# A planned attention stage: ten softmax norms on GpSimd, no mask products on TensorE, and a planner that ranks steps anew

## The chip, the core and the metric

One core of a Trainium2 chip runs the kernel. The metric is device microseconds (us) from the start to the end of one execution. Three runs of the kernel before took 621.08, 620.10 and 620.14 us, a median of 620.14.

## The reference

Three blocks follow one another, all in float32, for a batch of 4 and 576 positions:

```python
scores = scale * q @ k^T                       # 8 heads of 64
mask = (rel >= 0) & (rel < 64)                 # each position sees itself and 63 before it
attn = softmax(where(mask, scores, -1e9));  x = attn @ v            # x: 4 x 576 x 512

h = relu(x @ w_in);  u, vv = halves of h       # 512 -> 1024
vn = (vv - mean) / sqrt(var + 1e-6)            # over the 512 channels
x = (u * (w_spatial @ vn + b_spatial)) @ w_out

u = x + (relu(x^T @ w_tok1) @ w_tok2)^T
out = u + relu(u @ w_ch1) @ w_ch2              # 512 -> 1536 -> 512
```

The weights arrive as 8-byte floats and are turned into float32 on the chip, from their two 4-byte words.

## The kernel before

Matrix products of float32 quality are made of three products of halves: each operand is split into a rounded high part, made by ScalarE (a CAST), and a remainder, made by VectorE (a subtraction). So each tile that TensorE makes costs a ScalarE and a VectorE step before TensorE can use it again.

Attention runs in 18 turns (`its`), nine for each pair of batches; a turn holds 128 query rows of all 8 heads, and its softmax comes in two halves `g` of four heads. The steps of a turn, with the letters that the planner has for them: S, the scores on TensorE (`scores`, line 264); M, the row maxima on VectorE (`smax`, line 290); X, the exponentials with row sums on ScalarE (`sexp`, line 303); N, the reciprocal of the sums and the multiplication by it on VectorE (`snorm`, line 309); T, four transposes on TensorE (line 488); C, the copy of the transposed half out of the matmul bank on ScalarE (line 489); V, the product with the values (line 324); xh and xl, its split (lines 538 and 543).

For turns 0 to 5 (`MASK_PE = 6`) the mask is added by TensorE: a bf16 product of the identity with the mask (line 278) opens each of the two score banks, M is a reduction (line 294) and a scaling (line 301), and X reads the bank. For the others a fused VectorE instruction (line 297) adds the mask, writes the masked scores to SBUF and takes the minimum of the negated row; X then reads SBUF.

Behind the attention stand the first block's products: v and u (`uv_v_mm`, `uv_u_mm`) from the split x, with a ReLU (R, E), for v the normalisation (bn, rs on GpSimd, ts) and a split (hi, lo), then s, the spatial product, and G, its product with u (line 406). The weights `w_in` come in eight parts of 512 KB (four v, four u); each is loaded (wL), scaled by ScalarE (wd, line 136), joined by VectorE (wo, lines 439 and 440), and split (wh, line 443, and wl, line 445), all in a matmul bank that is held from wd to wl. Spatial, output and channel weights have like steps (`ws_load`, `wo_work`, `c2_work`); the last stores its halves to DRAM.

All of these are steps of a planner (`plan`, class `Steps`). Each step names its engine, a rank, a time in us, a hold (how long the engine is taken), the steps that it comes after, and what it takes and gives of rooms: `sp` (4 score banks), `xo`, `mm` (3 banks), `pb` (3 tiles of probabilities), `PT`, `v`, `qk`, `XT` and others. Steps with a `line` keep their order in that line. The planner simulates: it finds the engine and the earliest time at which some step can start, takes the step with the lowest rank among those of that engine that can start by then, and emits its instructions. So it fixes the order of instructions on each engine; the engines then run in that order and wait for one another with semaphores. Some 217 us of the run are planned in this way.

What follows is written out by hand: the other spatial products, the output product `W`, the token block (`T`, `A`, `tok2`), and the channel block in the form of seven products in place of eight (`ch1_seven`, `product`), with the preparation of weights in time slots beside it (`Line`, `bg`).

Of the kernel before, what the change touches and what calls it, by code (L numbers as in the profile page):

```python
# [25 lines left out]
MASK_PE = 6  # L26
# [3 lines left out]
PAIRS = 4  # L30
DOWN = 2.0 ** -112
# [7 lines left out]
class Steps:  # L39
# [5 lines left out]
    def __init__(self, **room):  # L45
        self.room = {k: [0.0] * n for k, n in room.items()}
        self.clock, self.done, self.open, self.lines = {}, {}, [], {}
        self.pad, self.queue, self.lands = 0, 0.0, [0.0] * 8
# [5 lines left out]
    def start(self, step):  # L54
        name, eng, rank, us, fn, after, take, give, hold, kb = step
        at = self.clock.get(eng, 0.0)
        for a in after:
            if a not in self.done:
                return None
            at = max(at, self.done[a] + self.LAG)  # L60
        for r in set(take):
            free, n = sorted(self.room[r]), take.count(r)
            if len(free) < n:
                return None
            at = max(at, free[n - 1] + self.LAG)
        return max(at, self.lands[-8 + (kb > 520)]) if kb else at

    def run(self):
        while True:
# [10 lines left out]
            gap = at - self.clock.get(eng, 0.0)  # L80
            self.pad = int((gap - 0.5) / 0.3) if PAD and eng == "PE" and gap > 0.8 and at < PAD else 0
# [16 lines left out]
def tile_kernel(ctx, tc, qT, kT, kE, v, w_in, wsT, b_sp, w_out, w_t1, w_t2, w_c1, w_c2, outT):  # L98
# [347 lines left out]

    def wu_part(ft):
        fs = slice(128 * ft, 128 * ft + 128)
        return w_part(U[:, ft, :1024], w_in[:, fs].rearrange("(k p) c -> p k c", p=P), wi_h[:, :, fs], wi_l[:, :, fs], 128)
# [10 lines left out]
    def plan():  # L460
# [11 lines left out]
        def attend(n):  # L472
# [8 lines left out]
            def turned(g):  # L481
# [7 lines left out]
                copies[n, g] = lambda: nc.scalar.copy(out=PT[0][:, 4 * g:4 * g + 4, :], in_=pt)  # L489

            for g in range(2):
                S.add(("M", n, g), "DVE", 1 + n / 100, 0.95, lambda g=g: smax(n, g), after=[("S", n)], give=free * (n >= MASK_PE))
                S.add(("X", n, g), "ACT", 2 + n / 100, 1.65, lambda g=g: sexp(n, g), after=[("M", n, g)], give=free * (n < MASK_PE), hold=1.54)
                S.add(("N", n, g), "DVE", 1 + n / 100, 1.15, lambda g=g: snorm(n, g), after=[("X", n, g)], hold=1.05)
                S.add(("T", n, g), "PE", 1 + n / 100, 0.65, lambda g=g: turned(g), after=[("N", n, g)], take=free + ["PT"] * (g == 0), give=["pb"] * g, line=("T", n), hold=0.45)
                S.add(("C", n, g), "ACT", 1, 0.6, lambda g=g: copies.pop((n, g))(), after=[("T", n, g)], give=free, hold=0.49)
# [7 lines left out]
        def score(n, after, line):  # L504
            S.add(("S", n), "PE", 0, 1.2 + 0.6 * (n < MASK_PE), lambda: scores(n), after=after + [("Lq", n), "ident"],
                  take=[] if after else ["sp", "sp", "pb"], give=["qk"], hold=1.0 + 0.6 * (n < MASK_PE), line=line)

        def block(ns):
# [16 lines left out]
            for m in ns:  # L525
                S.add(("V", m), "PE", 0, 1.25, lambda m=m: product(m), after=[("V", n)] if m > n else need,
                      take=take if m == n else [], give=["v", "PT"], hold=1.05, line=("B", n))
            for m in ahead:
                score(m, [("V", n)], ("B", n))
            for m in ns:  # L530
                S.add(("xh", m), "ACT", 0, 0.6, lambda m=m: xhigh(m), after=[("V", m)], hold=0.49)
                S.add(("xl", m), "DVE", 0, 0.7, lambda m=m: xlow(m), after=[("xh", m)], give=["mm" if m > n else "xo"], hold=0.6)
# [12 lines left out]
        def v_work(p, i):  # L545
# [15 lines left out]
            S.add(("v", n), "PE", 10, 2.9, product, after=[("xl", n)] + [("wl", "v", k) for k in range(4)], take=["mm"], hold=2.75, line="work")  # L561
            S.add(("R", n), "ACT", 1.5, 0.6, relu, after=[("v", n)], take=["vf"], give=["mm"], hold=0.49)
            S.add(("bn", n), "DVE", 2, 0.9, part, after=[("R", n)])
            S.add(("rs", n), "POOL", 0, 1.0, part, after=[("bn", n)])
            S.add(("ts", n), "DVE", 2, 0.56, part, after=[("rs", n)])
            S.add(("hi", n), "ACT", 4, 0.6 if i else 2.2, part, after=[("ts", n)])
            S.add(("lo", n), "DVE", 3, 0.7 if i else 1.3, part, after=[("hi", n)], give=["vf"])

        def u_work(p, c, ft):
            g = {}  # L570

            def product():
# [3 lines left out]
            S.add(("u", p, c, ft), "PE", 10, 2.25, product, after=[("xl", 9 * p + 3 * c + k) for k in range(3)] + [("wl", "u", ft)],  # L576
                  take=["mm"], give=["XT"] * (ft == 3), hold=2.09, line="work")
            S.add(("E", p, c, ft), "ACT", 1.5, 0.5 if c == 2 else 0.72, lambda: uv_u_out(p, c, ft, g["ps"]), after=[("u", p, c, ft)], give=["mm"])

        def s_work(b, d, c0):  # L580
# [8 lines left out]
            S.add(("s", b, d, c0), "PE", 10, 2.0, product, after=tiles + [("ws", k, c0) for k in range(6)], take=["mm"], hold=1.86, line="work")  # L589
            S.add(("G", b, d, c0), "DVE", 0.5, 0.47, lambda: spatial_out(b, d, c0, g["ps"]),  # L590
                  after=[("s", b, d, c0)] + [("E", p, c, d) for c in range(2 + b % 2)], give=["mm"], hold=0.4)

        def w_load(kind, k):
            it = (wv_part if kind == "v" else wu_part)(k)

            def part():
                next(it, 0)

            S.add(("wL", kind, k), "SP", 0, 0, part, hold=0.47, kb=512, line="SP")
            S.add(("wd", kind, k), "ACT", 1.8 if kind == "v" else 2.5, 0.7, part, after=[("wL", kind, k)], take=["mm"], hold=0.6)  # L600
            S.add(("wo", kind, k), "DVE", 0.8 if kind == "v" else 2.5, 1.25, part, after=[("wd", kind, k)])
            S.add(("wh", kind, k), "ACT", 1.8 if kind == "v" else 2.5, 0.6, part, after=[("wo", kind, k)], hold=0.49)
            S.add(("wl", kind, k), "DVE", 0.8 if kind == "v" else 2.5, 0.7, part, after=[("wh", kind, k)], give=["mm"], hold=0.6)

        def ws_load(k, c):
# [8 lines left out]
            S.add(("wh", k, c), "ACT", 3, 0.45, part, after=[("Lw", k, c)], hold=0.35)  # L614
            S.add(("ws", k, c), "DVE", 2.5, 0.45, part, after=[("wh", k, c)], give=["raw"], hold=0.38)
# [41 lines left out]
        def c2_work(j):  # L657

            rank = 6 + j
# [650 lines left out]
```

## Time and profile before

| what | value |
|---|---|
| median of three runs | 620.14 us |
| profiled execution | 621.39 us, of which the span is 619.5 us |
| busy: TensorE, VectorE, ScalarE, GpSimd | 97%, 76%, 57%, 19% of the span |
| mean granted clock of TensorE | 0.991 |
| instructions | 12149 |

The span is the time from the first to the last instruction that the profiler recorded. An engine is busy while it executes; waiting for a semaphore is idle time. TensorE's matmuls overlap one another, so its busy share can hide slow stretches; the number of matmuls in a stretch tells more. PE is TensorE, DVE VectorE, ACT ScalarE, POOL GpSimd, SP the engine that issues the DMAs.

### The profile page before, as it was taken

What the parts mean: (1) busy time and instruction counts of PE and PEld (TensorE: products, weight loads), DVE (VectorE), ACT (ScalarE), POOL (GpSimd) and SP (SyncE); (2) the same over time, 40 slices, a digit from 0 to 9 for tenths busy, and PEclk for the clock granted to TensorE, in tenths of its full rate; (3) what the DMA queues carried; (4) which work ended last, traced back from release to release, by engine and by line L of the source; (5) the groups of instructions that cost most, each with busy time, mean ns of one, the idle gap of its engine ahead of it and who ended that gap; (6) DMA issues with size and microseconds to landing.
All of it is one profiled execution on the core that took longest, in us unless ns stands there. A gap on an engine that the chain in (4) does not pass through costs nothing.

```text
span 619.5 us, 12149 instructions
## 1 busy us (share of the span) xinstructions
PE 600.2 (97%) x4396; PEld 560.6 (90%) x4396; DVE 472.6 (76%) x1066; ACT 352.7 (57%) x889; POOL 114.7 (19%) x145
## 2 busy tenths in 40 slices
PE   4999999999999989999999999999999999999997
PEld 2678899889988989788988999999999999999997
DVE  5998878968888836586278778888875989866982
ACT  5996786766777532674344454546443557544540
POOL 3000202302422200041025212140011140011320
PEclk8899999999999999999999999999999999999999
DMA  8956356866565652415200524665534674444752
GB/s 325 342 187 188 124 198 228 262 225 223 203 203 180 229 179 69 137 57 167 84 34 35 170 69 169 221 224 168 184 126 173 230 234 159 153 137 170 237 197 77
DMA packets 49812, 108.05 MB, mean 174 GB/s; under 512 B 4948, under 2 KB 17496, under 8 KB 49752
## 3 DMA queue, kind: packets, MB, share of 16 engines
q1 hardware_dynamic: 49752, 107.27, 51.2%
q8 instruction: 35, 0.57, 0.4%
q14 instruction: 25, 0.20, 0.1%
HBM read 86.81 MB, written 20.45 MB: 173 GB/s over the span
## 4 chain that ended last, share of the span: by engine, by line
PE 62%; DVE 4%; DMA 4%; ACT 2%; issue 1%; POOL 0%; ACTq 0%
PE A L1167 19%; PE mm L183 13%; PE mm L955 12%; PE A L955 9%; PE A L183 6%; DMA scr<-raw 3%; PE A L873 1%; DMA craw<-in_w_out 1%; PE A L1251 1%; DVE pb L297 1%; DVE raw L689 0%; ACT raw L686 0%; DVE pb L316 0%; DVE st L372 0%; DVE hid L949 0%
## 5 line engine op out<-in xcount | busy, mean ns | idle before, releaser
L1167 PE MATMUL A<-room,w 128*128 128x384 f32 x720 | 131.1, 335 | 0.7 <-DVE U L1203 0.7
L1167 PEld LDWEIGHTS A<-room,w 128*128 128x128 f32 x720 | 125.1, 188 | 2.1 <-DVE U L1203 1.0
L1161 ACT CAST room<-hid 128x384 fp32r<-128x384 f32 x120 | 61.3, 513 | 48.9 <-PE A L1167 37.5
L1162 DVE TENSOR_TENSOR room<-hid,room 128x384 fp32r<-128x384 f32 x120 | 71.9, 625 | 13.9 <-ACT room L1161 12.2
L949 POOL TENSOR_TENSOR hid<-hid 128x384 f32<-128x384 f32 x36 | 44.2, 1239 | 202.8 <-DVE hid L949 160.0
L183 PE MATMUL mm<-ws,room 128*128 128x288 f32 x416 | 61.0, 297 | 1.6 <-DVE U L406 1.5
L183 PEld LDWEIGHTS mm<-ws,room 128*128 128x128 f32 x416 | 56.7, 188 | 2.6 <-DVE U L406 2.1
L980 ACT ACTIVATE hid<-hid 128x384 f32<-128x384 f32 x54 | 28.1, 525 | 42.4 <-DVE hid L983 42.4
L983 DVE TENSOR_TENSOR hid<-A,hid 128x384 f32<-128x384 f32 x54 | 29.5, 554 | 24.7 <-PE A L955 18.4
L306 ACT ACTIVATE pb<-pb,nm 128x128 f32<-128x128 f32 x96 | 37.2, 392 | 2.8 <-DVE nm L297 2.8
L955 PE MATMUL mm<-room,sh 128*128 128x384 f32 x144 | 37.2, 334 | 0.0
L183 PE MATMUL mm<-xh,wi_h 128*128 128x384 f32 x96 | 33.2, 346 | 0.0
L183 PE MATMUL mm<-xh,wi_l 128*128 128x384 f32 x96 | 32.2, 336 | 0.0
L183 PE MATMUL mm<-xl,wi_h 128*128 128x384 f32 x96 | 32.2, 335 | 0.0
L1192 DVE TENSOR_TENSOR U<-A,U 128x384 f32<-128x384 f32 x42 | 21.9, 551 | 11.1 <-PE A L1167 6.5
L183 PE MATMUL mm<-gh,wo_h 128*128 128x512 f32 (+1 forms) x80 | 30.2, 378 | 0.0
L183 PE MATMUL mm<-gl,wo_h 128*128 128x512 f32 (+1 forms) x80 | 29.6, 370 | 0.2 <-DVE gl L855 0.2
L813 POOL TENSOR_TENSOR k<-k 128x256 f32<-128x256 f32 x12 | 9.7, 832 | 107.1 <-ACT gh L854 59.4
L183 PE MATMUL mm<-gh,wo_l 128*128 128x512 f32 (+1 forms) x80 | 29.5, 369 | 0.0
L855 DVE TENSOR_TENSOR gl<-U,gh 128x512 fp32r<-128x512 f32 (+1 forms) x20 | 13.3, 667 | 21.1 <-ACT gh L854 21.0
L488 PE MATMUL sp<-ident,pb 128*128 128x128 f32 x144 | 21.7, 284 | 7.0 <-DVE pb L316 3.0
L170 ACT CAST sh<-k 128x1024 fp32r<-128x1024 f32 x18 | 18.9, 1050 | 15.7 <-PE mm L955 5.9
(181 smaller groups left out, 1546.0 us busy)
## 6 DMA issues: line engine op xcount, KB each, us to landing
w<-scr SPq DMA_DIRECT2D x63, 512.0 KB, 4.1
scr<-raw SPq DMA_DIRECT2D x48, 256.0 KB, 3.5
k<-sums SPq DMA_DIRECT2D x18, 512.0 KB, 3.8
kk<-in_kT SPq DMA_DIRECT2D x16, 384.0 KB, 5.5
craw<-in_w_c SPq DMA_DIRECT2D x24, 256.0 KB, 3.7
qq<-in_qT SPq DMA_DIRECT2D x18, 256.0 KB, 5.5
va<-in_v SPq DMA_DIRECT2D x18, 256.0 KB, 4.4
vb<-in_v SPq DMA_DIRECT2D x18, 256.0 KB, 4.6
```

The lines of the kernel that those rows point to most:

```text
L170: nc.scalar.copy(out=hi, in_=x)
L183: nc.tensor.matmul(o, a, c, start=(i == 0), stop=(i == n - 1))
L306: nc.scalar.activation(out=pb[:, h, :], in_=scs[g][:, h - 4 * g, :] if mk is None else pb[:, h, :], func=AF.Exp, scale=SCALE if mk is None ...
L488: nc.tensor.transpose(pt[:, h, :], pb[:, 4 * g + h, :], ident)
L949: eng.tensor_tensor(out=out, in0=a, in1=b, op=ALU.subtract)
L955: nc.tensor.matmul(o, a, m, start=first and i == 0, stop=i == len(todo) - 1, skip_group_check=True)
L980: nc.scalar.activation(out=o, in_=src, func=AF.Relu)
L983: nc.vector.tensor_tensor(out=o, in0=a, in1=b, op=ALU.add)
L1161: nc.scalar.copy(out=oh, in_=blk[j])
L1162: nc.vector.tensor_tensor(out=ol, in0=blk[j], in1=f(oh), op=ALU.subtract)
L1167: nc.tensor.matmul(acc[d], a, m, start=(first and j == 0 and i == 0), stop=(last and j == NJ - 1 and i == 2), skip_group_check=True)
L1192: nc.vector.tensor_tensor(out=at, in0=src, in1=at, op=ALU.add)
```

## The change

The mask product goes from TensorE for all turns (`MASK_PE = 0`), so turns 0 to 5 have the fused VectorE instruction too. For turns 0 to 9 (`EARLY`) the multiplication by the reciprocal sum is done by GpSimd; the reciprocal stays on VectorE and becomes a step I of its own. For half 0 of turn 0 and half 1 of turns 3 to 7 (`CD0`, `CD1`) VectorE makes the copy C in place of ScalarE. One part of the u weights (`PU`) is prepared in place in SBUF, without a matmul bank, and its remainder is made by GpSimd. The order of the first fourteen loads changes (`ORDER`). In the planner all ranks are replaced by a table, several times and holds are changed, a step comes `SLACK` later behind the steps that it waits for (not behind rooms), and TensorE's clock in the simulation is charged `SWITCH` when it goes from one shape of matmuls to another. The hand-written part isn't changed.

```diff
-MASK_PE = 6
+MASK_PE = 0
+EARLY = range(0, 10)
+CD0 = range(0, 1)
+CD1 = range(3, 8)
+PU = (1,)
+ORDER = (0, 2, 5, 4, 3, 1, 7, 6, 10, 9, 8, 12, 13, 11)
+RANK = dict(M=0.96, X=5.22, I=-0.72, N=6.15, T=0.48, C=1.04, xh=3.48, xl=-0.6, R=0.29, bn=3.08, ts=0.44, hi=4.2, lo=5.8, E=1.49, G=-4.23, av=3.48, dv=1.82, au=4.89, du=3.49, aw=2.75, dw=1.67, c2=4.58)
+SLACK = dict(cd=0.38, cs=0.3, ch=2.95, cl=0.35, oh=0.73, ol=0.69, aw=2.46, ws=2.23, sums=0.17, wd=0, X=0, N=0.3, T=0.32, C=0.14, xh=0.03, xl=0.01, R=0.6, bn=1.03, ts=0.21, hi=0.54, lo=1.64, E=0.9, G=0.2)
+SHAPE = dict(S="score", V="pv")
+SWITCH = {(None, "pv"): 0.14, ("pv", "score"): 0.17, ("score", None): 0.28, ("pv", None): 0.16, (None, "score"): 0.2, ("score", "pv"): 0.14}
...
+        lag = self.LAG + SLACK.get(name[0], 0.0)
...
-            at = max(at, self.done[a] + self.LAG)
+            at = max(at, self.done[a] + lag)
...
+            if eng == "PE":
+                shape = SHAPE.get(name[0])
+                at += SWITCH.get((self.shape, shape), 0.0)
+                self.shape = shape
...
-        nc.vector.tensor_tensor(out=pb[:, hs, :], in0=pb[:, hs, :], in1=rs.unsqueeze(2).to_broadcast([P, w, 128]), op=ALU.mult)
+        yield
+        eng = nc.gpsimd if n in EARLY else nc.vector
+        eng.tensor_tensor(out=pb[:, hs, :], in0=pb[:, hs, :], in1=rs.unsqueeze(2).to_broadcast([P, w, 128]), op=ALU.mult)
...
+    def wu_pool(ft):
+        fs = slice(128 * ft, 128 * ft + 128)
+        raw = U[:, ft, :1024]
+        words = raw.rearrange("p (a c w) -> p a c w", a=4, w=2)
+        x, y, low = words[:, :, :, 1], words.bitcast(I32)[:, :, :, 1], words.bitcast(I32)[:, :, :, 0]
...
+        down(x, y)
+        yield
+        nc.vector.tensor_scalar(out=y, in0=y, scalar1=3, scalar2=None, op0=ALU.logical_shift_left)
+        nc.vector.scalar_tensor_tensor(out=y, in0=low, scalar=29, in1=y, op0=ALU.logical_shift_right, op1=ALU.bitwise_or)
+        yield
+        nc.scalar.copy(out=hi, in_=x)
+        yield
+        nc.gpsimd.tensor_tensor(out=lo, in0=x, in1=f(hi), op=ALU.subtract)
...
+                    if n in (CD0, CD1)[g]:
+                        nc.vector.tensor_copy(out=out, in_=pt)
+                    else:
+                        nc.scalar.copy(out=out, in_=pt)
...
-                S.add(("M", n, g), "DVE", 1 + n / 100, 0.95, lambda g=g: smax(n, g), after=[("S", n)], give=free * (n >= MASK_PE))
-                S.add(("X", n, g), "ACT", 2 + n / 100, 1.65, lambda g=g: sexp(n, g), after=[("M", n, g)], give=free * (n < MASK_PE), hold=1.54)
-                S.add(("N", n, g), "DVE", 1 + n / 100, 1.15, lambda g=g: snorm(n, g), after=[("X", n, g)], hold=1.05)
+                S.add(("M", n, g), "DVE", RANK["M"] + n / 100, 0.9, lambda g=g: smax(n, g), after=[("S", n)], give=free * (n >= MASK_PE))
+                S.add(("X", n, g), "ACT", RANK["X"] + n / 100, 1.8 if n >= MASK_PE else 1.6, lambda g=g: sexp(n, g), after=[("M", n, g)], give=free * (n < MASK_PE), hold=1.54 if n >= MASK_PE else 1.37)
+                early = n in EARLY
+                norm = snorm(n, g)
+                S.add(("I", n, g), "DVE", RANK["I"] + n / 100, 0.25, lambda norm=norm: next(norm), after=[("X", n, g)], hold=0.2)
+                S.add(("N", n, g), "POOL" if early else "DVE", RANK["N"] + n / 100, 1.45 if early else 0.8, lambda norm=norm: next(norm, 0), after=[("I", n, g)], hold=1.4 if early else 0.72)
...
-            S.add(("G", b, d, c0), "DVE", 0.5, 0.47, lambda: spatial_out(b, d, c0, g["ps"]),
+            S.add(("G", b, d, c0), "DVE", RANK["G"], 0.47, lambda: spatial_out(b, d, c0, g["ps"]),
...
+            S.add(("wl", kind, k), eng, d, 1.5 if pool_does else 0.7, part, after=[("wh", kind, k)], give=bank_of, hold=1.4 if pool_does else 0.6)
...
-        for fn, *a in ((load_queries, 0), (w_load, "v", 0), (load_queries, 1), (w_load, "v", 1), (load_values, 0), (w_load, "v", 2), (w_load, "v", 3),
-                       (load_queries, 2), (load_values, 1), (w_load, "u", 0), (load_queries, 3), (w_load, "u", 1), (w_load, "u", 2), (w_load, "u", 3)):
+        loads = ((load_queries, 0), (w_load, "v", 0), (load_queries, 1), (w_load, "v", 1), (load_values, 0), (w_load, "v", 2), (w_load, "v", 3),
+                 (load_queries, 2), (load_values, 1), (w_load, "u", 0), (load_queries, 3), (w_load, "u", 1), (w_load, "u", 2), (w_load, "u", 3))
+        for fn, *a in (loads[i] for i in ORDER):
```

## Rows read from the trace of the kernel before

**Rows 1.** The page: busy us, share of the span, instructions of each engine.
```profile
PE 600.2 (97%) x4396; PEld 560.6 (90%) x4396; DVE 472.6 (76%) x1066; ACT 352.7 (57%) x889; POOL 114.7 (19%) x145
```

**Rows 2.** TensorE's waits, whole run: engine, line waited for, total us, times, longest.
```profile
PE sc L278 <- POOL msk L115: 4.0, 1, 4.0
PE sp L488 <- DVE pb L316: 3.0, 3, 1.5
...
PE mm L183 <- DVE U L406: 1.5, 1, 1.5
PE sc L283 <- DMA kk<-in_kT: 1.0, 1, 1.0
PE mm L183 <- DVE wi_l L445: 1.0, 1, 1.0
...
```

**Rows 3.** Busy time of each engine by stretch, granted clock, DMA share, GB/s.
```profile
0.00:45.00 45.00, 33.94 (x411) 24.64 (x412) 36.44 (x86) 36.26 (x130) 5.97 (x23) 0.89 0.83 294
45.00:90.00 45.00, 44.96 (x478) 41.17 (x477) 39.01 (x143) 35.87 (x125) 5.55 (x11) 1.00 0.47 151
8.00:24.00 16.00, 11.72 (x120) 8.46 (x120) 15.45 (x34) 13.40 (x51) 0.00 (x0) 0.68 1.05 391
24.00:45.00 21.00, 18.56 (x257) 14.23 (x256) 20.11 (x51) 20.95 (x79) 1.26 (x4) 1.00 0.70 231
12.00:20.00 8.00, 5.88 (x64) 4.09 (x66) 7.79 (x16) 5.85 (x15) 0.00 (x0) 0.50 1.05 402
```

**Rows 4.** TensorE in order of time, 17 to 25 us: start, us, instructions.
```profile
17.86 1.03 PE L278 MATMUL sc<-msk,ident 128*128 128x512 bf16 x2
18.83 1.99 PE L283 MATMUL sc<-kk,qq 64*64 64x128 f32 x32
...
23.64 0.61 PE L278 MATMUL sc<-msk,ident 128*128 128x512 bf16 x2
24.17 1.10 PE L283 MATMUL sc<-kk,qq 64*64 64x128 f32 x32
```

**Rows 5.** VectorE's groups, 0 to 45 us: busy us, mean ns, idle before.
```profile
L294 DVE TENSOR_REDUCE mx<-sc 128x4 f32<-128x512 f32 x12 | 8.2, 684 | 7.1 <-PE sc L283 7.1
L316 DVE TENSOR_TENSOR pb<-pb,rs 128x512 f32<-128x512 f32 x11 | 7.6, 692 | 0.4
...
L301 DVE TENSOR_SCALAR nm<-mx 128x4 f32<-128x4 f32 x12 | 2.0, 170 | 0.4
```

**Rows 6.** The same view, 45 to 105 us.
```profile
L297 DVE CUSTOM_DVE_ANT_0 pb<-sc,msk 128x128 f32<-128x128 f32 x48 | 10.5, 286 | 0.0
```

**Rows 7.** ScalarE in order of time, about 8 and about 59 us.
```profile
8.07 0.37 ACT L306 ACTIVATE pb<-sc,nm 128x128 f32<-128x128 f32 x1 [0.63 <-DVE nm L301]
...
9.46 0.60 ACT L443 CAST wi_h<-mm 128x512 fp32r<-128x512 f32 x1
...
58.51 0.40 ACT L306 ACTIVATE pb<-pb,nm 128x128 f32<-128x128 f32 x1
...
60.06 0.25 ACT L344 ACTIVATE U<-mm 128x128 f32<-128x128 f32 x1
```

**Rows 8.** GpSimd's groups, whole run.
```profile
L949 POOL TENSOR_TENSOR hid<-hid 128x384 f32<-128x384 f32 x36 | 44.2, 1239 | 202.8 <-DVE hid L949 160.0 <-DVE room L1162 24.8 <-ACT sh L170 11.9
...
L937 POOL TENSOR_TENSOR k<-U,k 128x768 f32<-128x768 f32 x2 | 4.0, 1998 | 3.4 <-DVE U L895 3.4
```

**Rows 9.** TensorE's waits from 0 to 45 us.
```profile
PE sp L488 <- DVE pb L316: 1.5, 1, 1.5
```

**Rows 10.** VectorE in order of time behind the planned gate products.
```profile
221.02 0.29 DVE L630 TENSOR_SCALAR val<-val 128x256 int32<-128x256 int32 x1 [3.86 <-ACT val L136]
```

**Rows 11.** Two VectorE lines: durations min/median/max in ns (1162: 500.7 to 503.9 us).
```profile
L1162 DVE TENSOR_TENSOR room<-hid,room x5: 546/1366/1368, 500.1 to 503.8; 128x384 fp32r<-128x384 f32 x5
...
L983 DVE TENSOR_TENSOR hid<-A,hid x54: 542/557/558, 354.4 to 579.2; 128x384 f32<-128x384 f32 x54
```

**Rows 12.** GpSimd in order of time, 500.9 to 503.9 us.
```profile
501.01 3.78 POOL L949 TENSOR_TENSOR hid<-hid 128x384 f32<-128x384 f32 x3 [0.56 <-DVE room L1162]
```

More of the change, by code (lines that the diff above doesn't have):

```diff
@@ L46, in __init__ @@
         self.room = {k: [0.0] * n for k, n in room.items()}
-        self.clock, self.done, self.open, self.lines = {}, {}, [], {}
+        self.clock, self.done, self.open, self.lines, self.shape = {}, {}, [], {}, None
         self.pad, self.queue, self.lands = 0, 0.0, [0.0] * 8
@@ L505, in score @@
             S.add(("S", n), "PE", 0, 1.2 + 0.6 * (n < MASK_PE), lambda: scores(n), after=after + [("Lq", n), "ident"],
-                  take=[] if after else ["sp", "sp", "pb"], give=["qk"], hold=1.0 + 0.6 * (n < MASK_PE), line=line)
+                  take=[] if after else ["sp", "sp", "pb"], give=["qk"], hold=0.98 + 0.6 * (n < MASK_PE), line=line)
         def block(ns):
@@ L526, in block @@
                 S.add(("V", m), "PE", 0, 1.25, lambda m=m: product(m), after=[("V", n)] if m > n else need,
-                      take=take if m == n else [], give=["v", "PT"], hold=1.05, line=("B", n))
+                      take=take if m == n else [], give=["v", "PT"], hold=0.92, line=("B", n))
             for m in ahead:
@@ L530, in block @@
             for m in ns:
[L531 to L532 removed]
+                S.add(("xh", m), "ACT", RANK["xh"], 0.6, lambda m=m: xhigh(m), after=[("V", m)], hold=0.49)
+                S.add(("xl", m), "DVE", RANK["xl"], 0.7, lambda m=m: xlow(m), after=[("xh", m)], give=["mm" if m > n else "xo"], hold=0.6)
         def xhigh(n):
@@ L559, in part @@
                 next(g["it"], 0)
-            S.add(("v", n), "PE", 10, 2.9, product, after=[("xl", n)] + [("wl", "v", k) for k in range(4)], take=["mm"], hold=2.75, line="work")
-            S.add(("R", n), "ACT", 1.5, 0.6, relu, after=[("v", n)], take=["vf"], give=["mm"], hold=0.49)
-            S.add(("bn", n), "DVE", 2, 0.9, part, after=[("R", n)])
+            S.add(("v", n), "PE", 10, 2.95, product, after=[("xl", n)] + [("wl", "v", k) for k in range(4)], take=["mm"], hold=2.83, line="work")
+            S.add(("R", n), "ACT", RANK["R"], 0.6, relu, after=[("v", n)], take=["vf"], give=["mm"], hold=0.49)
+            S.add(("bn", n), "DVE", RANK["bn"], 0.9, part, after=[("R", n)])
             S.add(("rs", n), "POOL", 0, 1.0, part, after=[("bn", n)])
-            S.add(("ts", n), "DVE", 2, 0.56, part, after=[("rs", n)])
-            S.add(("hi", n), "ACT", 4, 0.6 if i else 2.2, part, after=[("ts", n)])
-            S.add(("lo", n), "DVE", 3, 0.7 if i else 1.3, part, after=[("hi", n)], give=["vf"])
+            S.add(("ts", n), "DVE", RANK["ts"], 0.56, part, after=[("rs", n)])
+            S.add(("hi", n), "ACT", RANK["hi"], 0.6 if i else 2.2, part, after=[("ts", n)])
+            S.add(("lo", n), "DVE", RANK["lo"], 0.7 if i else 1.3, part, after=[("hi", n)], give=["vf"])
         def u_work(p, c, ft):
@@ L574, in product @@
                 uv_u_mm(p, c, ft, g["ps"])
-            S.add(("u", p, c, ft), "PE", 10, 2.25, product, after=[("xl", 9 * p + 3 * c + k) for k in range(3)] + [("wl", "u", ft)],
-                  take=["mm"], give=["XT"] * (ft == 3), hold=2.09, line="work")
-            S.add(("E", p, c, ft), "ACT", 1.5, 0.5 if c == 2 else 0.72, lambda: uv_u_out(p, c, ft, g["ps"]), after=[("u", p, c, ft)], give=["mm"])
+            S.add(("u", p, c, ft), "PE", 10, 2.3, product, after=[("xl", 9 * p + 3 * c + k) for k in range(3)] + [("wl", "u", ft)],
+                  take=["mm"], give=["XT"] * (ft == 3), hold=2.17, line="work")
+            S.add(("E", p, c, ft), "ACT", RANK["E"], 0.5 if c == 2 else 0.72, lambda: uv_u_out(p, c, ft, g["ps"]), after=[("u", p, c, ft)], give=["mm"])
         def s_work(b, d, c0):
@@ L657, in c2_work @@
         def c2_work(j):
-            rank = 6 + j
+            rank = RANK["c2"] + j
             of = {}
```

30 lines of the change are left out of this document (19 added, 11 removed).

## The prediction

> **What bounds the kernel now.** I read the page first: TensorE is busy for 600.2 of 619.5 us [rows 1], so time can only come out of TensorE's own instructions, out of its 19.3 us of idling, or out of stretches in which it is busy but slow. Its list of waits comes second: 4.0 us are the start, 1.0 the second turn's keys, and nearly all the rest name a step that the planner places, a norm (line 316), a weight part (line 445), a gate product (line 406) [rows 2]. Third the stretches [rows 3]: in the first 45 us TensorE has 411 matmuls in 33.9 busy us, in the next 45 us 478 in 44.96. The reader is to see that the loss sits in the fill, that TensorE is full from 45 us on, and what limits the fill: VectorE is at work for 15.45 of 16 us from 8 to 24 and 20.1 of 21 from 24 to 45, ScalarE for 13.4 of 16 and then 20.95 of 21, and from 12 to 20 us TensorE's granted clock is 0.5 (1.2 GHz). What follows the planned part, some 400 us from about 217 us on, isn't edited.
>
> The sum is made against the profiled execution's own 621.39 us (span 619.5, and 1.89 around it). That execution is 1.25 us above the median of the three runs shown, 620.14; a gain in the span is taken off the median.
>
> **No mask products.** Twelve matmuls go, two for each of turns 0 to 5. A pair costs the step from its first matmul to the first score behind it [rows 4]: 0.97 us at 17.86 (half clock), 0.53 at 23.64, and 0.53 for each of two more pairs at 30 and 34 us that look like that one. Sum 2.6 us, where TensorE mostly goes from instruction to instruction. The pair at 6.97 us costs nothing, as the scores behind it wait for keys until 8.68. The pair at 3.99 goes too, but the scores then wait for their own loads, of which the trace shows only that they had landed by 5.05: 0 to 1.1 us, I take 0.5.
> In exchange VectorE adds the mask: four fused instructions at 10.5/48 us each, 0.88 a half [rows 6], for a reduction of 0.68 and a scaling of 0.17 [rows 5], so +0.02 us x 12 = 0.3 us. ScalarE's exponentials then read SBUF: four in 1.55 us (58.51 to 60.06) against 1.39 (8.07 to 9.46) [rows 7], +0.16 x 12 = 1.9 us. The score banks come free after the maximum, an exponential's 1.55 us sooner.
>
> **Ten turns' norms on GpSimd.** VectorE is rid of 20 multiplications of 0.69 us, 11 of them before 45 us: 7.6 us leave the fill [rows 5]. GpSimd's price for 128x512 isn't in the trace; 128x384 took 1.24 us and 128x768 2.0 [rows 8], so 1.49 on the line between them. Below lies 0.69, VectorE's own; above 1.65, the 384 row in proportion. Each such turn's chain grows by 1.49 - 0.69 = 0.8 us. GpSimd has nothing else from 8 to 24 us and 5.6 us of work from 45 to 90 [rows 3], so its queue delays the little rstd steps by at most one norm.
> **Copies and one weight part.** Six copies of turned tiles go from ScalarE (the planner holds it 0.49 us for one) to VectorE, three before 45 us: -1.5 us for ScalarE and, at the price of a norm, +2.1 for VectorE. Weight part 1 gives its last subtraction, 0.7 us by the same row, to GpSimd and takes no matmul bank. Its words lie in SBUF two apart, which can cost VectorE 0 to 0.7 us for each of two steps, once; I take 0.
> Net over the fill: VectorE -7.6 - 0.7 + 2.1 + 0.3 = -5.9 us of 36.4; ScalarE -1.5 + 1.9 = +0.4 of 36.3. That is the crux: of the two engines that limit the fill one is relieved, the other is not.
>
> **What it gives.** TensorE's idling in the fill is 45 - 33.9 = 11.1 us, without the start and the keys 6.1. VectorE ends 1.5 of it (a norm) [rows 9] and 1.0 (weights) [rows 2]; these 2.5 I let go. The other 3.6 are ended by ScalarE's steps, and I keep them, as ScalarE gets no lighter. Behind 45 us a norm is waited for twice more, 3.0 - 1.5 = 1.5 us [rows 2, 9]. Those turns keep VectorE's norm and change only their order: 0 to 1.5 us, I take half, 0.7.
> Slack and ranks cost no instruction, but a new order can also make late what was in time: up to 1.5 us lost by the same rows.
> At the end of the planned part VectorE stands for 3.86 us, in front of a joining of output weights [rows 10], and TensorE loses 1.5 at the next bank (line 406) [rows 2]. These loads start only when the last attention turn is done, so they move along with TensorE: 0 to 1.5 us gained, I take 0. The new load order at the start brings the second turn's queries ahead of the first weights. From 8 to 24 us the DMA engines are full, at 391 GB/s [rows 3], so what comes sooner makes something else later: I take 0, and a softmax step's 1.4 us either way as bounds.
> Sum: 2.6 + 0.5 + 2.5 + 0.7 = 6.3 us, and 620.14 - 6.3 = 613.8 us (own range 610 to 616.5).
>
> **A rule against it.** Where GpSimd subtracts without pause [rows 12], VectorE's subtractions of two SBUF tiles (line 1162) took 1366 ns in the median, and 546 at best; line 983, with one operand in PSUM, never took over 558 [rows 11]. Behind this stands the Trainium skill, "SBUF — State Buffer", section "Who interferes with whom": a VectorE instruction with two SBUF inputs and a GpSimd instruction that reads SBUF shut each other out for their whole length. The trace agrees. By that rule each norm on GpSimd can stop VectorE for up to a norm. How often it does follows from the code: of VectorE's steps in the fill, maxima, splits of products and weight words all have an operand in PSUM. From 45 to 105 us some 24 steps have two in SBUF (lines 384, 395, 167, 689, 631), while nine norms would take 9 x 1.49 = 13 of 60 us. If one in three collides at 0.4 us (half of 1366 - 546), that is 3 us, and VectorE has 6 us idle from 45 to 90 [rows 3]. I count nothing. Shut-outs that TensorE notices would be a part of rival D.
>
> **Rivals.**
> A, ScalarE is the fill's limit: its 20.95 of 21 us [rows 3] says so, and it gets 0.4 us more. Against it: TensorE idles for only 2.4 us of these 21. Then the waits just change their names and the masks alone are gained: 620.14 - 2.6 = 617.5.
> B, all stalls go: masks 2.6, start 1.1, fill 6.1, later 1.5, end 1.5: 12.8, so 607.3. For it: VectorE's queue has been full since 8 us, so ScalarE's steps that end a wait may themselves have stood behind it.
> C, given back: TensorE does its planned work sooner, and loses it again where the output weights and the channel weights are still being prepared, at the wait that is 1.5 us today. Then 620. Against it: the last of these loads start only when TensorE lets them.
> D, slower: the norm on GpSimd is late at the turn. TensorE takes its queue in order, so behind a turn that waits stand the products, and behind those the split of every later tile. If TensorE pays 0.8 us for half of the 11 norms before 45 us: +4.4 - 2.6 = +1.8. If it pays for all, at the upper bound of 1.65: 11 x 0.96 - 2.6 = +8.0. Middle 625 us. It decides as soon as TensorE has under 0.8 us of other work in front of each turn. Against it: a VectorE queue that is 5.9 us shorter starts each reciprocal sooner.
>
> **Numbers.** Forecast 0.42; A 0.14; B 0.15; C 0.10; D 0.19. A change under 0.2% (1.24 us) can't be told from none with this kernel. Faster: the forecast, A and B, 0.71; same: C, 0.10; slower: D, 0.19. The range runs from 607, just under B, to 621.5, near the mild end of D; it leaves out about 0.06 below and 0.14 above.
>
> **What would show it.** Right: the first 45 us hold over 420 matmuls that aren't masks (399 now), norm and weights are gone from TensorE's waits there, GpSimd's norms take 1.3 to 1.7 us, and all that follows the planned part is shifted by the gain. A shows as waits for exponentials and copies in their place; C as a longer wait for line 406; D as turns (line 488) that wait for GpSimd. The sum is wrong if the fill's idling wasn't what cost the time, or if turns gather behind GpSimd.

## The result, and the profile after

The changed kernel takes **615.21 us**, the median of 11 runs (614.47 to 619.32). The kernel before took 620.77 in the same rounds (11 runs, 620.1 to 622.38). The ratio is 0.9912, 95% interval 0.9895 to 0.9928: 5.5 us less by the ratio, 5.6 by the medians. The profiled executions, on which all readings of time below rest, took 615.11 us with a span of 613.3, and before 621.39 with a span of 619.5 [rows 1]: 6.2 us less in the span. Each trace shows a single execution.

The page of the kernel after: the span, and each engine's busy time.

```profile
span 613.3 us, 12221 instructions
PE 595.2 (97%) x4384; PEld 560.5 (91%) x4384; DVE 467.9 (76%) x1123; ACT 350.1 (57%) x883; POOL 137.6 (22%) x166
```

TensorE has twelve matmuls fewer and is busy for 5.0 us less; its idling went from 19.3 to 18.1 us. That reads as if the masks alone had done it. But a matmul at the lower clock counts as busy for longer: four transposes (line 522) take 1.12 us at 14.18 and 0.66 at 18.52. So the page alone can't say where the time came from. Its waits in the kernel after (engine, line waited for, us in total, times, longest):

```profile
PE sc L297 <- DMA kk<-in_kE: 4.9, 1, 4.9
PE sp L522 <- POOL pb L332: 4.0, 2, 3.5
PE sc L297 <- DMA kk<-in_kT: 2.8, 2, 1.8
PE sc L297 <- ACT PT L529: 1.0, 1, 1.0
PE sp L522 <- DVE pb L332: 0.9, 1, 0.9
PE A L1217 <- DVE U L1253: 0.7, 1, 0.7
...
```

Against [rows 2], the waits for the weight part and for line 406 are gone (its line is 422 now, and it isn't in the list). The norm on VectorE (line 332) went from 3.0 to 0.9 us. New is a wait of 3.5 us for a norm on GpSimd. The start is as long as before: the mask was waited for until 4.0, now the first scores wait for their keys until 4.9 (before, they began at 5.05, behind the masks).

The stretches of the kernel after: us, then PE, PEld, DVE, ACT and POOL busy, granted clock, DMA share, GB/s.

```profile
0.00:45.00 45.00, 32.31 (x410) 26.35 (x411) 34.79 (x154) 36.91 (x125) 18.25 (x34) 0.96 0.83 292
45.00:90.00 45.00, 45.00 (x486) 42.05 (x485) 37.09 (x133) 31.86 (x121) 14.59 (x19) 1.00 0.52 164
8.00:24.00 16.00, 9.70 (x146) 7.50 (x146) 13.56 (x63) 14.28 (x57) 4.38 (x5) 1.00 0.99 369
24.00:45.00 21.00, 20.64 (x232) 17.24 (x233) 20.25 (x84) 20.71 (x66) 9.14 (x11) 0.92 0.75 257
```

Against [rows 3], the fill holds 410 matmuls in place of 399 that weren't masks. TensorE's idling there went up, from 11.1 to 12.7 us; without the waits for the start and for keys it went from 6.1 to 5.0. VectorE got only 1.7 us lighter and not 5.9. The 48 fused steps cost about what the reductions and scalings did (10.7 against 10.2 us); but steps that came later before, among them three splits of spatial weights (1.7 us), now lie in these 45 us. The clock of 1.00 from 8 to 24 us is not to be trusted up to 18.26; the last section shows why.

Two tables say where the gain lies. The first is read straight from the two traces: the start of the first product of a kind, in us.

```
product on TensorE               before   after   difference
first u product                   44.52   42.64     -1.9
first spatial product             81.61   75.59     -6.0
ninth spatial product            128.70  122.86     -5.8
17th spatial product             209.43  205.39     -4.0
first output product             241.27  235.09     -6.2
first of the channel block       352.08  345.89     -6.2
```

All of the gain is made before the first output product, and nothing of it is given back or added later. In front of the first u product, the 17th spatial product and the first output product stand the same products in both kernels, masks aside, so these three rows are gain alone. In front of the first and the ninth spatial product they aren't the same, and those rows show order as well as gain. The second table takes that out: each planned matmul that has been issued counts with one duration for its kind, the same in both kernels, masks with none. The time less this work is what TensorE has lost so far.

```
time (us)     45     75     120    150    160    220    225
before      23.26  25.63  27.97  31.73  31.62  34.08  36.18
after       21.35  22.57  25.22  26.73  27.98  29.99  30.12
gained       1.9    3.1    2.8    5.0    3.6    4.1    6.1
```

Single columns swing by a us or two, as a product counts when it is issued. Both tables agree in the main: 1.9 us in the fill, some 2.2 from there to the last planned spatial products, and some 2.0 at the end of the planned part. How far such a start differs without any gain can be seen further down: the kernel with the copies back takes as long as the changed one, and its first u product starts at 42.10, 0.5 sooner.

### The profile page after: what moved, and what is told of

It reads as the page before. It is cut to its first block, busy times and chain, and to the rows that moved or that the text cites. A ratio compares the mean times of both kernels' runs of the same rounds, so it can differ in the third digit from the quotient of the medians.

```text
span 613.3 us, 12221 instructions
## 1 busy us (share of the span) xinstructions
PE 595.2 (97%) x4384; PEld 560.5 (91%) x4384; DVE 467.9 (76%) x1123; ACT 350.1 (57%) x883; POOL 137.6 (22%) x166
## 4 chain that ended last, share of the span: by engine, by line
PE 91%; DVE 3%; DMA 3%; ACT 2%; issue 1%; SPq 0%; POOL 0%; ACTq 0%; DVEq 0%
PE mm L197 33%; PE A L1217 20%; PE mm L1005 12%; PE A L1005 9%; PE A L197 6%; PE sc L297 3%; PE sp L522 2%; PE xo L340 2%; DMA scr<-raw 2%; PE A L923 1%; DMA kk<-in_kT 1%; PE mm L340 1%; PE A L1301 1%; DVE pb L311 1%; ACT pb L320 1%
## 5 line engine op out<-in xcount | busy, mean ns | idle before, releaser
L320 ACT ACTIVATE pb<-pb,nm 128x128 f32<-128x128 f32 x144 | 55.8, 392 | 7.6 <-DVE nm L311 7.4
L197 PEld LDWEIGHTS mm<-ws,room 128*128 128x128 f32 x416 | 56.8, 188 | 0.5 <-issue 0.3
L1033 DVE TENSOR_TENSOR hid<-A,hid 128x384 f32<-128x384 f32 x54 | 29.5, 553 | 24.6 <-PE A L1005 18.3
L311 DVE CUSTOM_DVE_ANT_0 pb<-sc,msk 128x128 f32<-128x128 f32 x144 | 31.5, 285 | 9.1 <-PE sc L297 9.1
L332 POOL TENSOR_TENSOR pb<-pb,rs 128x512 f32<-128x512 f32 x20 | 21.6, 1084 | 43.8 <-ACT pb L320 24.1
L1242 DVE TENSOR_TENSOR U<-A,U 128x384 f32<-128x384 f32 x42 | 21.9, 551 | 11.1 <-PE A L1217 6.5
L297 PE MATMUL sc<-kk,qq 64*64 64x128 f32 x576 | 21.6, 298 | 8.6 <-DMA kk<-in_kE 4.9
```

The lines of the kernel that those rows point to most:

```text
L197: nc.tensor.matmul(o, a, c, start=(i == 0), stop=(i == n - 1))
L297: nc.tensor.matmul(scs[e][64 * q:64 * q + 64, j, :], qq[er, j, 64 * q:64 * q + 64], kk[er, j, step * q:step * q + 128], start=not on_pe, s ...
L311: nc.vector.tensor_tensor_reduce(out=pb[:, 4 * g + h, :], in0=scs[g][:, h, :], in1=mk, scale=-SCALE, scalar=3e38, op0=ALU.add, op1=ALU.min ...
L320: nc.scalar.activation(out=pb[:, h, :], in_=scs[g][:, h - 4 * g, :] if mk is None else pb[:, h, :], func=AF.Exp, scale=SCALE if mk is None ...
L1033: nc.vector.tensor_tensor(out=o, in0=a, in1=b, op=ALU.add)
L1242: nc.vector.tensor_tensor(out=at, in0=src, in1=at, op=ALU.add)
```

## Experiments

"Order kept" means that every engine keeps the order of instructions of the kernel after; only then does a difference price one part. In the others the planner makes a new order.

**The masks back on TensorE**, order kept.

```diff
-        on_pe = n < MASK_PE
+        on_pe = n < 6
```

> The changed kernel (615.2 us) with the twelve mask products back on TensorE in front of the scores of turns 0 to 5, the order of every other instruction kept; the fused VectorE step stays, so the mask is added twice. Theory 1 (the prediction's sum: masks are 2.6 us of TensorE's path): 617.5 to 618.3. Theory 2 (order: in the changed kernel TensorE waits some 12 us before 26 us, so most pairs lie in waits and only the last two or three cost 0.53 each): 615.2 to 616.7.

617.53 us (616.89 to 619.42), ratio 0.9942 [0.9928, 0.9956]: some 2 us more than after. Its first u product starts at 43.25, 0.6 later than after's. So only 0.6 of the 2.6 us that I had put on the path shows there, at the end of the fill (1.1 against the 42.10 of the kernel with the copies back). The rest shows as waits further on (waits of this kernel's TensorE):

```profile
PE sp L522 <- DVE pb L332: 4.3, 3, 2.0
PE sc L292 <- POOL msk L129: 4.0, 1, 4.0
PE sp L522 <- POOL pb L332: 3.9, 2, 3.5
PE sc L292 <- ACT PT L529: 1.7, 1, 1.7
...
```

Line 332 on VectorE costs 4.3 us in place of 0.9. The profiled execution is the longest of the six, 1.9 us above their median, so these waits hold more than the median has. The time meets the theory that the masks cost what they take. The trace says otherwise: all masks are done before the first u product, and the rest of the 2 us comes behind it, from steps that come late.

**The ten turns' norms back on VectorE**, order kept.

```diff
-        eng = nc.gpsimd if n in EARLY else nc.vector
+        eng = nc.vector
```

> The changed kernel with the 20 early norms on VectorE, emitted at the same place, every other engine's order kept. Theory 1 (VectorE's relief shortens the fill): VectorE gets 20 x 0.69 us back, 10 of them before 45 us, and the time rises by 2.5 us or more, 617.7 to 621. Theory 2 (order): a norm on VectorE takes 0.69 instead of 1.04 us, so the first turns come sooner and the longer queue costs about as much: 614.7 to 616.5.

619.63 us (617.74 to 621.3, 12 runs), 0.9976 [0.9962, 0.999]: 4.0 us more than after by the ratios, 4.4 by the medians. Its first u product starts at 45.20, 2.6 later, and its first spatial product at 78.15, again 2.6 later; the first output product is 3.7 later. The waits of its TensorE:

```profile
PE sp L522 <- DVE rs L328: 5.8, 2, 4.3
...
PE sp L522 <- DVE pb L332: 2.5, 2, 1.8
PE sc L297 <- ACT PT L529: 1.2, 1, 1.2
PE xo L340 <- DVE xl L588: 1.0, 1, 1.0
...
```

The reader is to see VectorE's own steps (a reciprocal's first half, a norm, a split) back as the ones that end TensorE's waits. Of the three parts that were undone with the order kept (masks, norms, copies) this one costs the most. It is a price within an order made for norms on GpSimd. The weight part that is prepared without a matmul bank was not undone.

**No slack**, and **the old planner** with the new instructions (old ranks, no slack, no switches, old load order; the steps' times and holds as changed).

```diff
-SLACK = dict(...)
+SLACK = {}
```

> The changed kernel planned without any slack; ranks, switches, load order and instructions as changed. Theory 1 (slack costs and brings nothing to speak of): 614.5 to 616. Theory 2 (the order makes the later gain: the waits of 1.3, 0.5 and 2.1 us that were in the kernel before between 120 and 224 us are gone through slack): they come back in part, 616.5 to 619.

```diff
+RANK = dict(M=1, X=2, I=1, N=1, T=1, C=1, xh=0, xl=0, R=1.5, bn=2, ts=2, hi=4, lo=3, E=1.5, G=0.5, ...)
+SLACK = {}
+SWITCH = {}
+ORDER = range(14)
```

> The changed kernel's instructions (no masks on TensorE, ten norms on GpSimd, six copies on VectorE, one weight part without a bank) planned with the ranks and the load order of before, without slack and switches; times and holds of the steps as changed. Theory 1 (the relief brings the gain): 615 to 617. Theory 2 (the order brings it): 618.5 to 622.

Without slack 629.04 us (627.69 to 632.11), 1.0139 [1.0115, 1.0163]: 14 us more than after, slower than before, and outside both expectations. With the old planner 622.02 (620.55 to 625.39, 12 runs), 1.0018 [1.0001, 1.0034]: no gain at all from the new instructions. TensorE's waits, first without slack, then with the old planner:

```profile
PE sp L522 <- POOL pb L332: 10.4, 8, 3.5
...
PE sp L522 <- ACT vf L383: 2.8, 1, 2.8
PE mm L197 <- ACT xh L583: 1.7, 1, 1.7
...
```

```profile
PE sp L522 <- POOL pb L332: 7.0, 5, 4.8
...
PE sp L522 <- ACT pb L320: 1.1, 1, 1.1
PE xo L340 <- ACT PT L529: 1.1, 2, 0.6
PE mm L197 <- DVE U L422: 1.0, 1, 1.0
...
```

This is rival D: turns waiting for a norm on GpSimd. Of the eight waits two, 4.0 us, stand in front of the first turn, and the changed kernel has these too; the other six, 6.4 us, appear only without slack. My reading, not tested by itself: they appear once the planner puts a turn's transposes where GpSimd's norm is only just due by its own arithmetic. With the old planner the wait at the end (line 422, 406 before) is back too.

**The old ranks with slack, switches and load order.**

```diff
-RANK = dict(...)
+RANK = dict(M=1, X=2, I=1, N=1, T=1, C=1, xh=0, xl=0, R=1.5, ...)   # as before
```

> The changed kernel planned with the ranks of before, but with slack, switches and the new load order; the run with none of these took 622.0 us. Theory 1 (slack makes an order robust under any ranks): 616 to 620. Theory 2 (slack is worth nothing of itself, the picked combination is): 621 to 632.

619.79 us (618.11 to 621.56), 0.9974 [0.9955, 0.9992]: 2 to 3 us better than the old planner whole, and some 4 worse than after. The end's wait (U, 1.3 us) and a wait of 4.8 for GpSimd stay. So slack, switches and load order together bring 2 to 3 us to the old ranks, and the new ranks some 4 on top. These prices don't simply add: slack taken from under the new ranks costs 14 us.

**Other instructions, and an order planned for them**, in three forms: the changed kernel with its norms on VectorE and planned so; the new planner over all the instructions of before; and the kernel before, with its own planner, with only its masks taken off TensorE. In the first two the norm on VectorE also gets the rank of the reciprocal's step; that line isn't shown.

```diff
-EARLY = range(0, 10)
+EARLY = range(0)
...
```

> The changed kernel with the early norms on VectorE and the planner told so (0.8 us, hold 0.72, rank of the reciprocal's step); everything else as changed. Theory 1 (VectorE has no room for 20 norms in the fill, in whatever order): 618 to 621. Theory 2 (a planner that knows finds an order as good): 615 to 617.

```diff
-MASK_PE = 0
+MASK_PE = 6
-EARLY = range(0, 10)
-CD0 = range(0, 1)
-CD1 = range(3, 8)
-PU = (1,)
+EARLY = CD0 = CD1 = range(0)
+PU = ()
...
```

> The new planner (ranks, slack, switches, load order, times) over the instructions of before: masks on TensorE, all norms on VectorE, all copies on ScalarE, all weight parts in matmul banks. Theory 1 (the relief brings the gain): 619 to 624. Theory 2 (the order brings it): 615.5 to 618.

```diff
 (the kernel before)
-MASK_PE = 6
+MASK_PE = 0
```

> The kernel before with its mask products gone and nothing else changed; its own planner knows of it. Theory 1 (2.6 us of TensorE's path): 617.5 to 619. Theory 2 (in an order made for other times the masks' time turns into waits, as ScalarE's exponentials get 1.9 us longer): 619.5 to 623.

630.15 us (1.0147 [1.0124, 1.017]), 631.42 (1.0169 [1.0144, 1.0195]) and 629.13 (1.014 [1.0115, 1.0165]): all three 8 to 11 us slower than before, and all three above both of their expectations. None loses it in a single stall: behind the start the longest are 4.3, 2.7 and 2.7 us, where the changed kernel has one of 3.5. TensorE in order of time in the third, the kernel before without masks (start, us, instructions, idle before and what ended it):

```profile
37.13 0.63 PE L488 MATMUL sp<-ident,pb 128*128 128x128 f32 x4 [0.87 <-DVE nm L297]
...
39.81 0.46 PE L324 MATMUL xo<-PT,va 128*64 128x64 f32 x3 [1.21 <-ACT PT L489]
...
42.91 1.09 PE L488 MATMUL sp<-ident,pb 128*128 128x128 f32 x4 [1.76 <-ACT pb L306]
...
45.85 2.11 PE L488 MATMUL sp<-ident,pb 128*128 128x128 f32 x8 [1.86 <-DVE rs L314]
...
49.67 1.08 PE L488 MATMUL sp<-ident,pb 128*128 128x128 f32 x4 [1.72 <-ACT wi_h L443]
50.41 2.05 PE L183 MATMUL mm<-wi_h,xh 128*128 128x512 f32 x4
```

Turn after turn comes late, by 0.9 to 1.9 us in these rows, each time for another step; the first u product starts at 56.8 in place of 44.5. A second loss goes with the waits: the granted clock is 0.5 (1.2 GHz) from 41.98 to 55.63, and four matmuls of a v product take 2.05 us, where the changed kernel needs 1.17 (at 28.99). TensorE is busy for 9.15 us of that stretch. If half of it is lost to the clock, that is an estimated 4.6 of the 8.3 us. The first of the three has such a stretch from 38.10 to 48.34 (busy for 8.20 us, so an estimated 4.1). Instructions were taken off the busiest engine, and the kernel got 8 us slower because the planner answered with another order. These runs therefore don't price the masks or the norms. They show how far another order, with the waits and the clock that it brings, can move the time. Nor do they show that the new planner is poor with other instructions as such: its ranks and slacks are those of the change, and no others were tried with these instructions.

**The six copies back on ScalarE**, order kept.

```diff
-                    if n in (CD0, CD1)[g]:
+                    if False:
```

> The changed kernel with the six copies of turned tiles back on ScalarE, emitted at the same place, all other order kept. Theory 1 (both engines limit the fill, a copy on the wrong one costs): three copies of 0.49 us in a full ScalarE queue before 45 us, +0.5 to +1.5, 615.7 to 616.7. Theory 2 (they balance out): 615 to 615.6.

615.45 us (614.89 to 615.74), 0.9907 [0.9892, 0.9923]: the same as after. The copies are worth nothing that these runs can show.

**The start's chain shortened**, and with it one norm moved ahead of a step that can stand behind a store. A table names steps that are emitted ahead of another step; all else is as in after.

```diff
-            fn()
+            hoisted(self, name, fn)      # emits HOIST[name] first
+HOIST = {("wd", "v", 2): [M(0,0), X(0,0), M(0,1), X(0,1)], ("M", 1, 0): [M, X, I and N of (0,0) and (0,1)]}
+HOIST[("cl", 2, 7)] = [("N", 15, 1)]     # only in the second
```

> The changed kernel with two places of the start turned round and no other order touched: the second half's exponentials of turn 0 ahead of the first weight part on ScalarE, and turn 0's two reciprocals ahead of turn 1's maxima on VectorE. The first turn's transposes, which waited 3.5 us for GpSimd until 14.18, can come at about 10.7. Theory 1 (the chain of turn 0 is on TensorE's path): 612.5 to 614.3. Theory 2 (the first v product at 29 us waits for weights and places in the order, so a sooner first turn only makes a longer wait later): 614.6 to 615.6.

> The changed kernel with the two hoists of the start and a third: on VectorE the norm of turn 15's second half ahead of a channel weight's remainder that waits for ScalarE, which waits for a store. That norm cost TensorE 0.93 us at 152 us in the changed kernel and 1.64 with the start hoisted alone. Theory 1 (what TensorE waits for is what the time consists of): the 0.5 us of the fill stay and 0.9 to 1.6 us come on top, 613.3 to 614.5. Theory 2 (the wait moves to the next turn behind the same store): 614.8 to 616.4.

616.37 us (615.26 to 616.96), 0.9928 [0.9906, 0.995], above both expectations, and 614.18 (613.22 to 614.76), 0.9888 [0.9871, 0.9904]. The first turn's transposes in after, and in the first of these two:

```profile
14.18 1.12 PE L522 MATMUL sp<-ident,pb 128*128 128x128 f32 x4 [3.50 <-POOL pb L332]
15.75 1.12 PE L522 MATMUL sp<-ident,pb 128*128 128x128 f32 x4 [0.45 <-POOL pb L332]
```

```profile
10.68 1.12 PE L522 MATMUL sp<-ident,pb 128*128 128x128 f32 x4 [1.63 <-POOL pb L332]
12.18 1.12 PE L522 MATMUL sp<-ident,pb 128*128 128x128 f32 x4 [0.38 <-POOL pb L332]
```

The turn comes 3.5 us sooner, yet the first u product only 0.5 (42.14 against 42.64): the longest new wait in the list is worth a seventh of its length at most. It may be worth nothing, as the kernel with the copies back has its first turn at 13.11 and its first u product at 42.10 with the start untouched. And at 152 us a wait of 0.93 in after is one of 1.64 in the first of these two; the second kernel takes it away. In after that wait is this, on ScalarE, VectorE and TensorE in turn:

```profile
149.57 0.41 ACT L735 CAST raw<-cy 128x256 fp32r<-128x256 f32 x1 [2.46 <-DMA scr<-raw]
...
150.01 0.42 DVE L738 TENSOR_TENSOR raw<-cy,raw 128x256 fp32r<-128x256 f32 x1 [2.31 <-ACT raw L735]
...
151.03 0.68 DVE L332 TENSOR_TENSOR pb<-pb,rs 128x512 f32<-128x512 f32 x1
...
151.87 0.63 PE L522 MATMUL sp<-ident,pb 128*128 128x128 f32 x4 [0.93 <-DVE pb L332]
```

A cast of channel weights waits until an earlier half has been stored to DRAM; its subtraction waits on VectorE, and a norm stands behind it in VectorE's queue. The planner adds slack to steps that come after a late one, but not to a tile that has to be given back. With that norm moved ahead of the subtraction, VectorE does it at 148.59, in front of the standing step, and TensorE doesn't notice (VectorE, then TensorE, in the second kernel):

```profile
148.59 0.69 DVE L332 TENSOR_TENSOR pb<-pb,rs 128x512 f32<-128x512 f32 x1
149.88 0.42 DVE L738 TENSOR_TENSOR raw<-cy,raw 128x256 fp32r<-128x256 f32 x1 [0.60 <-ACT raw L735]
...
150.16 1.47 PE L522 MATMUL sp<-ident,pb 128*128 128x128 f32 x12
```

**A neighbouring order.** The planner's time for a hand-over between engines is 10 ns longer; hundreds of places in the order change.

```diff
-LAG = 0.1
+LAG = 0.11
```

> The changed kernel with the planner's assumed delay between two steps at 0.11 in place of 0.10 us, ranks, slack and instructions as changed: another order from the same rules. Theory 1 (the rules make the order good): 614.5 to 617. Theory 2 (this order is good because it was picked among many, and its neighbours are not): 620 to 632.

613.51 us (612.37 to 615.72), 0.9883 [0.986, 0.9905]. This one neighbour is at least as good, and its time lies below the lower bound that was expected. So the order in the change isn't good by luck alone. This kernel, which has no wait at 152 us either, and the second of the two before it have the lowest times of all that ran; their intervals overlap with after's, so only the gain over before is certain for them.

## Why the prediction was right, and where it wasn't

**Sign and size** came out: 6.3 us were forecast, 5.5 measured (6.2 in the profiled spans). The terms did not, and the total is in good part luck: the fill brought 1.9 of its 5.6 us, and 1.5 more than forecast between 45 and 220 us and 2.0 at the end made up for it. Of the four signs named, two failed: the fill holds 410 matmuls and not over 420, and GpSimd's norms take 1.08 us and not 1.3 to 1.7. In the fill VectorE's norm and the weights did go from TensorE's waits, and what follows the planned part is shifted by the gain.

- **Masks, 2.6 us on the path in the fill: over-sized.** Put back they cost 2.0 in all, but the path only 0.6 in the first 43 us. I counted the pairs at 17 to 34 us as path because TensorE "mostly goes from instruction to instruction" there. But TensorE idled for 4.3 us from 8 to 24 us and for 2.4 from 24 to 45 [rows 3]; a mask pair that ends ahead of such a moment only fills it. (This reading is argued; the 0.6 is measured.) The masks also gave something back: with them on TensorE the second turn's scores take 1.10 us (8.68 before, 8.47 with the masks back), without them 1.98 (8.70), as the last section shows.
- **Start, 0.5: came to 0.2.** The scores waited for their keys instead (4.88 against 5.05).
- **Fill waits ended by VectorE, 2.5: right in size**, by the kernel with the norms back at the same places: 2.6 us at the first u product, though in the new order and for the norms alone. Yet the whole fill gained 1.9 where 5.6 was forecast. The undone parts sum to 3.2 (2.6 and 0.6), so by that sum about 1.3 was lost on the way, with a first turn that comes 2.9 us later (14.18; in the trace of before that group starts at 11.26). Its reciprocals stand on VectorE behind the second turn's maxima, which wait for keys that land at 8.6 and for the scores that take 0.9 us longer. Shortening that chain by 3.5 us brought back 0.5 at most; the rest I can't place.
- **GpSimd's norm, 1.49 us: over-sized.** It takes 1.08. GpSimd's groups of the kernel after, 0 to 110 us:

```profile
L332 POOL TENSOR_TENSOR pb<-pb,rs 128x512 f32<-128x512 f32 x20 | 21.6, 1084 | 43.8 <-ACT pb L320 24.1 <-DVE rs L329 18.1 <-ACT mm L150 0.7
...
L479 POOL TENSOR_TENSOR wi_l<-U,wi_h 128x512 fp32r<-128x512 f32 x1 | 1.3, 1310 | 0.0
```

  So a turn's chain grows by 0.4, not by 0.8. I had drawn the line through subtractions of two full tiles. The norm's second operand is one value for each head's row, and the weight part's subtraction of two full tiles did take 1.31 (one instruction, one of whose tiles lies two words apart; what makes the difference wasn't tested).
- **Later waits, 0.7: under-sized**, 2.2 from 45 to 220 us. The stalls at 128.3 and 145.9 us of before are gone, and one of 0.93 has come at 152. That makes 0.9 us; the list of waits doesn't show the rest.
- **The end, 0: wrong.** I looked at the loads alone, which do move along with TensorE: the last two are issued 3.2 and 1.4 us ahead of the 21st spatial product before, 3.6 and 2.3 us now. What changed is VectorE's order. The kernel has three matmul banks for these products, so the 23rd product needs the bank that the gate product of the 20th gives back. Before, that gate product stood behind the joining of [rows 10], which waits for a load (VectorE, then TensorE):

```profile
221.69 0.45 DVE L406 TENSOR_TENSOR U<-mm,U 128x288 f32<-128x288 f32 x1
...
222.19 1.98 PE L183 MATMUL mm<-ws,room 128*128 128x288 f32 x13 [1.48 <-DVE U L406]
```

  In the kernel after it stands in front of the joining, which still waits, and the 23rd product doesn't (VectorE, VectorE, TensorE):

```profile
213.01 0.46 DVE L422 TENSOR_TENSOR U<-mm,U 128x288 f32<-128x288 f32 x1 [0.81 <-PE mm L197]
216.29 0.29 DVE L679 TENSOR_SCALAR val<-val 128x256 int32<-128x256 int32 x1 [2.83 <-ACT val L150]
...
216.53 1.87 PE L197 MATMUL mm<-ws,room 128*128 128x288 f32 x13
```

  The kernel with the masks back bears this out: its joining comes as late as before, 4.2 us behind the start of the 21st product (221.36 and 217.14; before 221.02 and 216.84), but behind the same gate product, and its 23rd product doesn't wait. Under the old ranks (both runs) the joining is in front again, and so is the wait. Rival C put a loss here; it was a gain of 2.0.
- **"Slack and ranks cost no instruction ... up to 1.5 us" is the step that failed**, although the total hides it. The new instructions under the old planner gain nothing (622.0), the new planner over the old instructions loses 10 us (631.4), and without slack the change loses 8 (629.0). Among the runs made, only both together gain. The order is the larger term by far, some 15 us between orders of the same instructions, where the prediction had bounded it by 1.5 us lost or gained. A bound from single waits of one good order couldn't show that: the order before was itself one that had come out well, as the 629.1 us of the kernel before without masks suggest.
- **Rivals.** A (ScalarE remains the limit) is half true: ScalarE was busy for 20.71 of 21 us from 24 to 45, and waits for its copy (1.0) appear, but giving it six copies back costs nothing. D was the right danger. Its condition, under 0.8 us of other work in front of each turn, is what the slack guards against by my reading, and without slack D happens: 10.4 us of waits, 6.4 more than with it.
- **The rule of the Trainium skill** that the prediction cites did come true, without harm here. In the kernel after, norms on GpSimd stretch ten steps of VectorE, at 29 us and from 47 to 90, by some 6 us in sum against the same lines where GpSimd is idle, twice the 3 us of the estimate. None of TensorE's listed waits falls between 24.4 and 151 us. (Line 1212, 1162 before, has the same rate in both kernels, from other work on GpSimd: 24 of its 120 subtractions meet a GpSimd instruction and take 0.92 us in the mean, the other 96 take 0.55.)

**Open:** why orders without slack, or planned for other instructions, come out 8 to 14 us slower as a group is shown only by their waits and by the clock behind them; which of the slacks matters wasn't taken apart, nor were the switches, the load order and the weight part without a bank priced alone. A further store buffer, which would remove the wait at 152 us at its cause, wasn't tried.

## What to carry to other kernels

Where a program writes the order of in-order queues, price an edit with the order kept; replanned, its price drowns in that of the order (here 2 and 4 us, in some 15 between orders of the same instructions). Plan slack for whatever ends on a DMA or a slow engine, also where the DMA only gives a buffer back, and compare the order with a neighbour before believing it. Of a long wait in a list ask what stands behind it: here 3.5 us in front of the first turn were worth 0.5 at most. And of a load that comes late ask what stands behind its step in the queue: here the order of two VectorE steps, not the load, made the 1.5 us at the end.

## What the runs showed of the hardware

Single-operand steps of VectorE were stretched too while GpSimd worked. The prediction had counted only steps with two SBUF operands. One line of the kernel after, with its shortest, median and longest duration in ns:

```profile
L394 DVE TENSOR_SCALAR vf<-vf,mv,rstd x18: 517/546/1412, 39.1 to 202.1; 128x512 f32<-128x512 f32 x18
```

Ten of these 18 meet no GpSimd instruction and take 541 ns in the mean; the eight that do take 983. Line 328, four columns, takes 163 ns in the median and at most 1008. The fused step of line 311, which reads a score bank, takes 286 ns alone and 284 with GpSimd at work. "SBUF — State Buffer" of the Trainium skill, "Who interferes with whom", names this form (tensor_scalar) among those that can take the ports shared with GpSimd where their operands meet some conditions. The trace agrees as far as the stretching goes.

The start of the clock's record has to be checked against the matmuls. The trace of the kernel after has its first record of the clock at 18.26 us, and the view prints 1.00 for the time ahead of it; but the matmuls there are as slow as at 0.5 (1.2 GHz). TensorE in the kernel after, and the second turn's scores in the kernel before:

```profile
8.70 1.98 PE L297 MATMUL sc<-kk,qq 64*64 64x128 f32 x32 [1.83 <-DMA kk<-in_kT]
...
14.18 1.12 PE L522 MATMUL sp<-ident,pb 128*128 128x128 f32 x4 [3.50 <-POOL pb L332]
...
18.52 0.66 PE L522 MATMUL sp<-ident,pb 128*128 128x128 f32 x4
```

```profile
8.68 1.10 PE L283 MATMUL sc<-kk,qq 64*64 64x128 f32 x32 [0.98 <-DMA kk<-in_kT]
```

Before, the record has 1.0 from 7.24 to 10.65, behind masks and scores that kept TensorE at work from 3.99 to 7.69, then 0.5 until 20.89. In the kernel after TensorE works from 4.88 to 6.86 and waits until 8.70, and its matmuls are slow until about 18.3; the record has 0.5 again from 25.09 to 28.50. So nothing here shows that the change gained by the clock. For the same reason the mean granted clock of an execution can't be compared between runs here: the time ahead of its first record counts as 1.0 in it. What the clock costs in the fill of either kernel wasn't measured apart.
